# Five of twelve gate/val chunks computed with seven products instead of eight

## The chip, the cores and the metric

The kernel runs on 1 core of one Trainium2 chip. The metric is device time in microseconds (us) of one execution; three runs of the kernel before stand below. Engines are named as in the profile: PE (TensorE, its weight loads as PEld), DVE (VectorE), ACT (ScalarE), POOL (GpSimd), SP (the queue that issues the loads).

## What is computed

Causal attention of 24 (batch, head) pairs, 448 tokens, head dimension 64, in all 896 tokens of 768 features, and then two feed-forward blocks. The inputs of the blocks are fp64.

```python
def _moe_ref(x, w_in, w_out):            # 768 -> 2048 -> 768
    h = x @ w_in
    g = np.where(h >= 1, h, np.where(h <= -1, 0.0, (h + 1) ** 2 / 4))
    return (g @ w_out).astype(np.float32)

def _moe2_ref(x, w_gate, w_val, w_out):  # 768 -> 1536 -> 768
    g = x @ w_gate
    return (g / (1.0 + np.exp(-g)) * (x @ w_val) @ w_out).astype(np.float32)
```

## The kernel before

The kernel goes through five stages, each held on chip: attention (with the first part of x @ w_in woven in), the rest of h, y = g @ w_out ("Y stage", 6 column chunks d), gate and val with u = silu(gate)·val ("gv stage", 12 column chunks f, two groups g of N = 448 tokens), and u @ w_o2 (output stage, two halves hf, 7 token tiles, 6 weight pieces).

Every large product is made exact enough by splitting both operands into a high and a low part (fp32r): mm3 issues three matmuls, high·high, high·low, low·high. A gv chunk is 2 (gate, val) × 2 token groups × 6 contraction pieces × 3 = 72 matmuls of 128 rows by 448 columns, each with its own weight load. `split` makes the parts of an activation: a cast on ACT (L84) and a subtraction on DVE (L85). y is split as each of its column chunks ends (L515), u at the end of each chunk and token group (L541).

Weights come as 768-column pieces by one queue of loads (SP, L100). The class Weights turns a piece into high and low parts in a generator, `operations`: three integer steps on DVE (L116, L123, L127) put the fp32 number together from the fp64 bits, ACT casts the high part (L135), and POOL subtracts for the low part (L136; DVE for the first nine pieces). `tick` advances this by one step, `get` runs it until a piece is there, `free` gives a buffer back; four buffers (WBUFS) are in rotation.

At the start PE runs products of zeros (`zeros`, L382): WARM = 18 ahead of the first scores, and HOLD = (12, 6, 4, 2) more in the first turns of the attention loop. The scores of a step (`scores`) are matmuls of q and k, then matmuls that add the mask; DVE takes their maximum next (`greatest`, L277).

A scheduler orders the instructions of each engine by a priority that falls with the place in the program; each engine then runs its list in order. `follow` keeps matmuls of one group together, and PINNED holds the first weight steps in program order.

## Time and profile before

| | us |
|---|---|
| three runs | 621.1, 620.0, 621.09 |
| median | 621.09 |
| the profiled execution | 620.53 |
| its span | 618.8 |
| PE busy (matmul records) | 608.1 |
| PEld busy | 533.2 |
| DVE busy | 361.1 |
| ACT busy | 210.5 |
| POOL busy | 117.8 |

The busy times are sums of one execution over its span. A matmul's record begins before the one ahead of it has ended, so the records of PE overlap, and their sum is not the time that PE needs at its closest spacing. The profiled execution's own time is the span and what lies around it, 1.7 us.

### The profile page before, as it was taken

To read this page: it belongs to the slowest core of one execution; us is meant where nothing else is said; L and a number is where in the kernel's file an instruction comes from. 1 tells how busy PE (TensorE), PEld (TensorE's weight loads), DVE (VectorE), ACT (ScalarE), POOL (GpSimd) and SP (SyncE) were. 2 spreads that over 40 slices of the span, in tenths; PEclk is the share of its full clock that TensorE was granted. 3 is DMA by queue.
4 is the path that set the end of the run, shared out by engine and by line. 5 is a ranking of instruction groups with operands and counts; after the bars stand their busy time and mean duration, and the time that the engine had idled before them with its cause. 6 is when DMAs were issued, how large, how long until landed. Compare 5 with 4: busy or idle time off the path is not lost.

```text
span 618.8 us, 8656 instructions
## 1 busy us (share of the span) xinstructions
PE 608.1 (98%) x3394; PEld 533.2 (86%) x3398; DVE 361.1 (58%) x687; ACT 210.5 (34%) x455; POOL 117.8 (19%) x68
## 2 busy tenths in 40 slices
PE   9999999999999999999999999999999999999997
PEld 4666667668999999999999999999999999999997
DVE  2999999773796766443344455555555555532401
ACT  3777877563344433111111322222222222112100
POOL 0000000000311222232232322222222223321300
PEclk9999999999999999999999999999999999999999
DMA  7576554200140233422333333333333333335002
GB/s 238 160 223 192 178 171 153 68 0 2 47 157 14 94 101 111 126 101 86 126 113 112 120 94 127 111 103 106 110 124 120 103 103 103 103 110 172 14 0 90
DMA packets 18665, 67.81 MB, mean 110 GB/s; under 512 B 2112, under 2 KB 6784, under 8 KB 18624
## 3 DMA queue, kind: packets, MB, share of 16 engines
q1 hardware_dynamic: 18624, 67.25, 34.3%
q8 instruction: 27, 0.44, 0.3%
q14 instruction: 14, 0.11, 0.1%
HBM read 64.49 MB, written 2.75 MB: 109 GB/s over the span
## 4 chain that ended last, share of the span: by engine, by line
PE 87%; DVE 10%; ACT 3%; issue 0%; ACTq 0%
PE mm L73 62%; PE mm L556 5%; PE mm L555 5%; PE mm L554 5%; PE mm L75 3%; DVE s L277 2%; ACT p L291 2%; PE s L73 2%; DVE p L315 2%; PE o L75 1%; PE t L75 1%; PE mm L382 1%; DVE wt L123 1%; PE s L75 1%; PE o L73 1%; DVE wt L127 1%
## 5 line engine op out<-in xcount | busy, mean ns | idle before, releaser
L136 POOL TENSOR_TENSOR wl<-wt,wh 128x768 fp32r<-128x768 f32 (+1 forms) x61 | 116.9, 1918 | 470.5 <-ACT wh L135 470.5
L135 ACT CAST wh<-wt 128x768 fp32r<-128x768 f32 (+1 forms) x70 | 57.3, 819 | 179.2 <-PE mm L73 108.8
L73 PE MATMUL mm<-yh,wl 128*128 128x448 f32 x288 | 105.3, 366 | 0.0
L73 PE MATMUL mm<-yh,wh 128*128 128x448 f32 x288 | 105.3, 365 | 0.0
L73 PE MATMUL mm<-yl,wh 128*128 128x448 f32 x288 | 105.2, 365 | 0.0
L116 DVE TENSOR_SCALAR wt<-wraw 128x768 int32<-128x768 int32 (+1 forms) x70 | 41.4, 591 | 109.0 <-POOL wl L136 108.8
L73 PE MATMUL mm<-gh,wh 128*128 128x448 f32 x192 | 70.2, 365 | 0.0
L73 PE MATMUL mm<-gh,wl 128*128 128x448 f32 x192 | 70.2, 365 | 0.0
L73 PE MATMUL mm<-gl,wh 128*128 128x448 f32 x192 | 70.2, 365 | 0.0
L123 DVE SCALAR_TENSOR_TENSOR wt<-wraw,wt 128x768 int32<-128x768 int32 (+1 forms) x70 | 67.4, 964 | 1.3
L127 DVE SCALAR_TENSOR_TENSOR wt<-wraw,wt 128x768 int32<-128x768 int32 (+1 forms) x70 | 65.2, 931 | 1.6
L73 PE MATMUL mm<-xh,wh 128*128 128x448 f32 x165 | 62.5, 379 | 2.2 <-DVE q L200 2.1
L73 PEld LDWEIGHTS mm<-yh,wh 128*128 128x128 f32 x288 | 54.1, 188 | 4.2
L73 PEld LDWEIGHTS mm<-yl,wh 128*128 128x128 f32 x288 | 54.1, 188 | 4.2
L73 PEld LDWEIGHTS mm<-yh,wl 128*128 128x128 f32 x288 | 54.1, 188 | 4.2
L555 PE MATMUL mm<-wl,uh 128*128 128x384 f32 x168 | 56.2, 334 | 0.0
L556 PE MATMUL mm<-wh,ul 128*128 128x384 f32 x168 | 56.2, 334 | 0.0
L554 PE MATMUL mm<-wh,uh 128*128 128x384 f32 x168 | 56.2, 334 | 0.0
L291 ACT ACTIVATE p<-s,mx 112x112 f32<-112x112 f32 (+3 forms) x96 | 46.3, 495 | 23.2 <-DVE mx L279 17.9
L73 PE MATMUL mm<-xl,wh 128*128 128x448 f32 x138 | 50.4, 365 | 0.0
L73 PE MATMUL mm<-xh,wl 128*128 128x448 f32 x138 | 50.2, 365 | 0.0
L277 DVE TENSOR_REDUCE s<-s 112x2 f32<-112x224 f32 (+3 forms) x48 | 35.0, 736 | 8.9 <-PE s L75 8.6
(73 smaller groups left out, 945.5 us busy)
## 6 DMA issues: line engine op xcount, KB each, us to landing
wraw<-w_gv SPq DMA_DIRECT2D x24, 768.0 KB, 4.2
wraw<-w_in SPq DMA_DIRECT2D x16, 768.0 KB, 4.4
wraw<-w_out SPq DMA_DIRECT2D x12, 768.0 KB, 4.4
wraw<-w_o SPq DMA_DIRECT2D x12, 768.0 KB, 4.2
qk_t<-qk SPq DMA_DIRECT2D x12, 336.0 KB, 4.5
wraw<-w_out SPq DMA_DIRECT2D x6, 512.0 KB, 3.8
qk_t<-qk SPq DMA_DIRECT2D x12, 224.0 KB, 2.9
v_t<-v SPq DMA_DIRECT2D x12, 224.0 KB, 2.7
```

What stands on the lines that cost most here:

```text
L73: return product(*args, **kw)
L75: return tc.keep_in_program_order(product(*args, **kw))
L116: first = nc.vector.tensor_scalar(out=t, in0=w[:, :, 1], scalar1=3, scalar2=0x3FFFFFF8, op0=ALU.logical_shift_left, op1=ALU.bitwise_and,)
L123: nc.vector.scalar_tensor_tensor(out=t, in0=w[:, :, 1], scalar=-0x40000000, in1=t, op0=ALU.bitwise_and, op1=ALU.bitwise_or,)
L127: nc.vector.scalar_tensor_tensor(out=t, in0=w[:, :, 0], scalar=29, in1=t, op0=ALU.logical_shift_right, op1=ALU.bitwise_or,)
L135: nc.scalar.copy(out=wh[:, :n], in_=t.bitcast(F32))
L136: (nc.vector if i < LOW_V else nc.gpsimd).tensor_tensor(out=wl[:, :n], in0=t.bitcast(F32), in1=wh[:, :n].bitcast(F32), op=ALU.subtract,)
L277: nc.vector.tensor_reduce(out=mx[:, i], in_=s[:C, :, off:off + w], axis=AX.X, op=ALU.max)
L291: nc.scalar.activation(out=p[:, h, off:off + w], in_=s[:C, h, off:off + w], func=AF.Exp, bias=mx[:, i, h:h + 1], scale=0.125, accum_out=sm ...
L554: nc.tensor.matmul(out=ps, lhsT=c, rhs=a, start=(f == 0), stop=False)
L555: nc.tensor.matmul(out=ps, lhsT=c, rhs=b, start=False, stop=False)
L556: nc.tensor.matmul(out=ps, lhsT=d, rhs=a, start=False, stop=(f == FC2 - 1))
```

## The change

In five of the twelve chunks (SEVEN = 2, 4, 6, 8, 10) the gate and val of both token groups and both halves of the contraction are computed by one level of Strassen's scheme, in the form with seven products (`seven`); the other chunks keep eight (`eight`). A product is 3 contraction pieces × 3 matmuls = 9 matmuls of 448 columns. The scheme needs sums:

- Of the weights: four sums of 384 columns on DVE (`sums`), and parts of three of their blocks (768, 384, 384 columns), cast on ACT and subtracted on DVE (S_LOW = "V"). POOL subtracts the low part of half of val.
- Of y: T1 to T4, three pieces each, on DVE. The raw y is copied to SBUF by ACT in the Y stage, and the parts of y and of the T are made at the end of that stage.
- Of the products: c1, c5 (copies on ACT), c16, c167 and three more additions on DVE in each such chunk.

u is kept unsplit; its parts are made (`split_u`) for f = 0, 1 behind chunk 10 and for the others in the first half of the output stage. WARM goes from 18 to 8. The first step of 24 gv weight pieces is kept in program order.

```diff
--- before.py
+++ after.py
...
-WARM = 18
+WARM = 8
...
+SEVEN = (2, 4, 6, 8, 10)
...
+S_LOW = "V"
...
-                if i < PINNED:
+                if i < PINNED or PIN0 <= i - I_GV < PIN1:
                     tc.keep_in_program_order(first)
...
+                f, val = divmod(i - I_GV, 2)
+                if f in SEVEN and i < I_O2:
+                    if not val:
+                        gate = t.bitcast(F32)
+                    else:
+                        yield from self.sums(i, gate, t.bitcast(F32))
+                        continue
...
+        def sums(self, i, gate, val):
+
+            g, v = ([x[:, k * HALF:(k + 1) * HALF] for k in range(2)] for x in (gate, val))
+            wh = wp.tile([128, WB], F32R, tag="wh", name="vh")
+            wl = wp.tile([128, WB], F32R, tag="wl", name="vl")
+            nc.scalar.copy(out=wh[:, :HALF], in_=v[1])
+            nc.gpsimd.tensor_tensor(out=wl[:, :HALF], in0=v[1], in1=wh[:, :HALF].bitcast(F32), op=ALU.subtract)
+            t = sums_p.tile([128, 4 * HALF], F32, tag="s", name="ws", bufs=1)
+            sh = sums_p.tile([128, 3 * HALF], F32R, tag="sh", name="sh")
+            sl = sums_p.tile([128, 3 * HALF], F32R, tag="sl", name="sl")
+            s1, s2, s3, s4 = (t[:, k * HALF:(k + 1) * HALF] for k in range(4))
+            nc.vector.tensor_tensor(out=s1, in0=v[0], in1=v[1], op=ALU.add)
+            nc.vector.tensor_tensor(out=s2, in0=s1, in1=g[0], op=ALU.subtract)
+            yield
+            nc.vector.tensor_tensor(out=s4, in0=g[1], in1=s2, op=ALU.subtract)
+            nc.vector.tensor_tensor(out=s3, in0=g[0], in1=v[0], op=ALU.subtract)
+            yield
+            for hi, lo, x in ((sh[:, :WB], sl[:, :WB], t[:, :WB]), (sh[:, WB:], sl[:, WB:], s3),
+                              (wh[:, HALF:], wl[:, HALF:], s4)):
+                nc.scalar.copy(out=hi, in_=x)
+                (nc.vector if S_LOW == "V" else nc.gpsimd).tensor_tensor(
+                    out=lo, in0=x, in1=hi.bitcast(F32), op=ALU.subtract)
+                if x is not s4:
+                    yield
+            self.got[i] = wh, wl, sh, sl
+            self.ready = i + 1
+            yield
+
...
-    for g in range(2):
-        Y[g] = (xy.tile([128, KC, N], F32R, tag="xh", name="yh"), xy.tile([128, KC, N], F32R, tag="xl", name="yl"))
+
+    raw = [xy.tile([128, KC, N], F32, tag="xh", name="yraw") for g in range(2)]
+    sums12, sums34 = (xy.tile([128, KC, N], F32, tag="xl", name="traw") for _ in range(2))
+    T1, T2, T3, T4 = sums12[:, :3], sums12[:, 3:], sums34[:, :3], sums34[:, 3:]
     for d in range(KC):
         pss = [bank() for _ in range(2)]
...
+        if d == KC - 1:
+            break
+        ps = [p[:, :N] for p in pss]
         for g in range(2):
-            split(pss[g][:, :N], Y[g][0][:, d], Y[g][1][:, d])
+            nc.scalar.copy(out=raw[g][:, d], in_=ps[g])
+        e = d - 3
+        if d < 3:
+            nc.vector.tensor_tensor(out=T1[:, d], in0=ps[1], in1=raw[0][:, d], op=ALU.subtract)
+        else:
+            nc.vector.tensor_tensor(out=T2[:, e], in0=ps[1], in1=T1[:, e], op=ALU.subtract)
+            nc.vector.tensor_tensor(out=T3[:, e], in0=ps[1], in1=raw[1][:, e], op=ALU.subtract)
+            nc.vector.tensor_tensor(out=T4[:, e], in0=ps[0], in1=T2[:, e], op=ALU.subtract)
     gctx.close()
-
-    up = ctx.enter_context(tc.tile_pool(name="up", bufs=1, reuse_waits="tile"))
-    uh = [up.tile([128, 2 * N], F32R, tag=f"uh{f}", name=f"uh{f}") for f in range(FC2)]
-    ul = [up.tile([128, 2 * N], F32R, tag=f"ul{f}", name=f"ul{f}") for f in range(FC2)]
-    for f in range(FC2):
-        ws = [W.get(I_GV + 2 * f), W.get(I_GV + 2 * f + 1)]
+    mctx = ExitStack()
+    yp = mctx.enter_context(tc.tile_pool(name="yp", bufs=1, reuse_waits="tile"))
+    sums_p = mctx.enter_context(tc.tile_pool(name="sums_p", bufs=2, reuse_waits="tile"))
+    tctx = ExitStack()
+    tp = tctx.enter_context(tc.tile_pool(name="tp", bufs=1, side="right", reuse_waits="tile"))
+    Y = {(g, c): [yp.tile([128, N], F32R, name=f"y{part}{g}_{c}") for part in "hl"] for c in range(KC) for g in range(2)}
+    for g in range(2):
+        for c in range(KC - 1):
+            split(raw[g][:, c], *Y[g, c])
+        split(pss[g][:, :N], *Y[g, KC - 1])
+    ps = [p[:, :N] for p in pss]
+    nc.vector.tensor_tensor(out=T2[:, 2], in0=ps[1], in1=T1[:, 2], op=ALU.subtract)
+    nc.vector.tensor_tensor(out=T3[:, 2], in0=ps[1], in1=raw[1][:, 2], op=ALU.subtract)
+    nc.vector.tensor_tensor(out=T4[:, 2], in0=ps[0], in1=T2[:, 2], op=ALU.subtract)
+    T = {}
+    for k, t in enumerate((T1, T2, T3, T4)):
+        T[k] = [tp.tile([128, 3, N], F32R, name=f"t{part}{k}") for part in "hl"]
+        split(t, *T[k])
+
...
+    def add(ps, w, at, rows, first, last):
+
+        for c in range(3):
+            sl = slice(at + c * 128, at + (c + 1) * 128)
+            for i, (a, b) in enumerate(((0, 0), (0, 1), (1, 0))):
+                nc.tensor.matmul(
+                    out=ps[:, :N], lhsT=w[a][:, sl], rhs=rows[c][b], start=(first and c == i == 0),
+                    stop=(last and c == i == 2), skip_group_check=True,
+                )
+
+    def gated(f, g, gate, val):
+        sg = ev.tile([128, N], F32, tag="r", name="sg")
+        nc.scalar.activation(out=sg, in_=gate, func=AF.Sigmoid)
+        nc.vector.tensor_tensor(out=sg, in0=gate, in1=sg, op=ALU.mult)
+        nc.vector.tensor_tensor(out=u_raw[f][:, g * N:(g + 1) * N], in0=val, in1=sg, op=ALU.mult)
+
+    def eight(f, ws):
         for g in range(2):
-            yh, yl = Y[g]
-            pss = []
+            pss = [bank() for _ in range(2)]
             for s in range(2):
-                wh, wl = ws[s]
-                ps = bank()
-                for c in range(KC):
-                    sl = slice(c * 128, (c + 1) * 128)
-                    mm3(ps[:, :N], wh[:, sl], wl[:, sl], yh[:, c], yl[:, c], c == 0, c == KC - 1)
-                pss.append(ps)
+                for half in range(2):
+                    add(pss[s], ws[s], half * HALF, chunks(g, half), not half, bool(half))
+                    W.tick(TICK8[half])
                 if g:
                     W.free(I_GV + 2 * f + s)
-            sg = ev.tile([128, N], F32, tag="r", name="sg")
-            nc.scalar.activation(out=sg, in_=pss[0][:, :N], func=AF.Sigmoid)
-            nc.vector.tensor_tensor(out=sg, in0=pss[0][:, :N], in1=sg, op=ALU.mult)
-            u = pss[1][:, :N]
-            nc.vector.tensor_tensor(out=u, in0=u, in1=sg, op=ALU.mult)
-            split(u, uh[f][:, g * N:(g + 1) * N], ul[f][:, g * N:(g + 1) * N])
-            W.tick(4)
+            gated(f, g, *(p[:, :N] for p in pss))
+
+    def seven(f, ws):
+
+        gate, val, sums = ws[0], ws[1][:2], ws[1][2:]
+        b1, b2, b3 = (bank() for _ in range(3))
+        p1, p2, p3 = (b[:, :N] for b in (b1, b2, b3))
+        c1, c5 = (ev.tile([128, N], F32, tag="t", name=f"c{i}") for i in (1, 5))
+        c16, c167 = (ev.tile([128, N], F32, tag="c", name=f"c{i}") for i in (16, 167))
+        add(b1, gate, 0, chunks(0, 0), True, True)
+        nc.scalar.copy(out=c1, in_=p1)
+        W.tick(1)
+        add(b2, sums, HALF, sums_of(1), True, True)
+        nc.vector.tensor_tensor(out=c16, in0=p2, in1=c1, op=ALU.add)
+        W.tick(1)
+        add(b3, sums, 0, sums_of(0), True, True)
+        nc.scalar.copy(out=c5, in_=p3)
+        W.tick(1)
+        add(b1, gate, HALF, chunks(0, 1), False, True)
+        W.free(I_GV + 2 * f)
+        W.tick(1)
+        add(b2, sums, 2 * HALF, sums_of(2), False, True)
+        nc.vector.tensor_tensor(out=c167, in0=p2, in1=c1, op=ALU.add)
+        W.tick(1)
+        add(b3, val, HALF, chunks(1, 1), False, True)
+        nc.vector.tensor_tensor(out=p3, in0=p3, in1=c16, op=ALU.add)
+        nc.vector.tensor_tensor(out=c5, in0=c5, in1=c167, op=ALU.add)
+        gated(f, 1, p3, c5)
+        W.tick(1)
+        add(b2, val, 0, sums_of(3), False, True)
+        W.free(I_GV + 2 * f + 1)
+        nc.vector.tensor_tensor(out=p2, in0=p2, in1=c1, op=ALU.add)
+        gated(f, 0, p1, p2)
+        W.tick(2)
+
+    u_raw, uh, ul = {}, {}, {}
+
+    def split_u(pool, f):
+        uh[f], ul[f] = (pool.tile([128, 2 * N], F32R, name=f"u{part}{f}") for part in "hl")
+        for g in range(2):
+            half = slice(g * N, (g + 1) * N)
+            split(u_raw[f][:, half], uh[f][:, half], ul[f][:, half])
+
+    for f in range(FC2):
+        if f % 3 == 0:
+            triple = xy.tile([128, KC, N], F32, tag=("xh", "xl")[f // 3 % 2], name="u")
+            for e in range(3):
+                u_raw[f + e] = triple[:, 2 * e:2 * e + 2].rearrange("p g n -> p (g n)")
+        ws = [W.get(I_GV + 2 * f), W.get(I_GV + 2 * f + 1)]
+        (seven if f in SEVEN else eight)(f, ws)
+        if f == SEVEN[-1]:
+            tctx.close()
+            up = ctx.enter_context(tc.tile_pool(name="up", bufs=1, side="right", reuse_waits="tile"))
+            for e in range(2):
+                split_u(up, e)
+    mctx.close()
+    up2 = ctx.enter_context(tc.tile_pool(name="up2", bufs=1, reuse_waits="tile"))
...
         last = NB - LASTB
         for i in range(last):
             w = W.get(I_O2 + hf * NB + i)
+            if hf == 0:
+                for f in range(2 * i + 2, 2 * i + 4):
+                    split_u(up if f < 6 else up2, f)
             for t in range(7):
                 product(i, w, t)
...
```

**PE at the start.** The kernel before, from the last of its 18 zeros; s_144 and s_167 are the scores of the first two steps, mask_b and ident_b the mask and the identity that adds it:

```order
L382 MATMUL mm_114<-idle_112 128x512
L73 MATMUL s_144<-qk_t_100 112x224 [waits DMAHW0_49]
L75 MATMUL s_144<-qk_t_100 112x224
L75 MATMUL s_144<-qk_t_100 112x112 x2
L73 MATMUL s_167<-qk_t_104 112x224 [waits DMAHW2_49]
L75 MATMUL s_167<-qk_t_104 112x224
L75 LDWEIGHTS ident_b_59 [waits DVE_49]
L75 MATMUL s_144<-mask_b_60,ident_b_59 112x112 [waits Pool_49]
L75 MATMUL s_167<-qk_t_104 112x112
```

The kernel after, from the last of its 8 zeros; s_134 and s_157 are the same scores:

```order
L421 MATMUL mm_114<-idle_112 128x512
L77 MATMUL s_134<-qk_t_100 112x224 [waits DMAHW0_49]
L79 MATMUL s_134<-qk_t_100 112x224
L79 MATMUL s_134<-qk_t_100 112x112 x2
L77 MATMUL s_157<-qk_t_104 112x224 [waits DMAHW2_49]
L79 MATMUL s_157<-qk_t_104 112x224
L79 MATMUL s_157<-qk_t_104 112x112 x2
L421 LDWEIGHTS idle_112
```

The scores of both steps now stand together behind 8 zeros; 7 more zeros (of HOLD) follow, and then the eight mask matmuls, which before stood among the scores.

**DVE in the gv stage.** Before, a token group's end; wt is a weight piece in its three steps, sg and mm the gate and u, ul the low part of u:

```order
L127 SCALAR_TENSOR_TENSOR wt_3730<-wraw_3626,wt_3730 128x768 [waits DVE_49]
L540 TENSOR_TENSOR mm_3597<-mm_3597,sg_3616 128x448 [waits PE_49]
L116 TENSOR_SCALAR wt_3784<-wraw_3680 128x768 [waits DMAHW3_49,Pool_49]
L85 TENSOR_TENSOR ul1_3415<-mm_3597,uh1_3403 128x448 [waits Activation_49]
L123 SCALAR_TENSOR_TENSOR wt_3784<-wraw_3680,wt_3784 128x768 [waits DVE_49]
L127 SCALAR_TENSOR_TENSOR wt_3784<-wraw_3680,wt_3784 128x768 [waits DVE_49]
L538 TENSOR_TENSOR sg_3670<-mm_3632,sg_3670 128x448 [waits Activation_49]
L540 TENSOR_TENSOR mm_3651<-mm_3651,sg_3670 128x448 [waits DVE_49,PE_49]
L85 TENSOR_TENSOR ul2_3416<-mm_3651,uh2_3404 128x448 [waits Activation_49]
```

After, a chunk of seven products, from the last u of the chunk before it:

```order
L608 TENSOR_TENSOR u_3773<-mm_3838,sg_3887 128x448 [waits PE_49]
L632 TENSOR_TENSOR c16_3896<-mm_3892,c1_3894 128x448 [waits PE_49,Activation_49]
L120 TENSOR_SCALAR wt_3922<-wraw_3811 128x768 [waits DMAHW5_49]
L127 SCALAR_TENSOR_TENSOR wt_3922<-wraw_3811,wt_3922 128x768 [waits DVE_49]
L131 SCALAR_TENSOR_TENSOR wt_3922<-wraw_3811,wt_3922 128x768 [waits DVE_49]
L641 TENSOR_TENSOR c167_3897<-mm_3892,c1_3894 128x448 [waits PE_49]
L645 TENSOR_TENSOR c5_3895<-c5_3895,c167_3897 128x448 [waits DVE_49,Activation_49]
L644 TENSOR_TENSOR mm_3893<-mm_3893,c16_3896 128x448 [waits PE_49]
L607 TENSOR_TENSOR sg_3972<-mm_3893,sg_3972 128x448 [waits Activation_49]
L650 TENSOR_TENSOR mm_3892<-mm_3892,c1_3894 128x448 [waits PE_49]
```

The subtraction of u's low part is gone from this stage. The three weight steps stand between c16, which waits for the second product, and c167, which waits for the fifth.

**DVE where the Y stage ends.** Before; yl is the low part of the last column chunk of y, one for each token group:

```order
L116 TENSOR_SCALAR wt_3382<-wraw_3306 128x768 [waits DMAHW5_49,Pool_49]
L123 SCALAR_TENSOR_TENSOR wt_3382<-wraw_3306,wt_3382 128x768 [waits DVE_49]
L127 SCALAR_TENSOR_TENSOR wt_3382<-wraw_3306,wt_3382 128x768 [waits DVE_49]
L116 TENSOR_SCALAR wt_3514<-wraw_3352 128x768 [waits DMAHW6_49,Pool_49]
L123 SCALAR_TENSOR_TENSOR wt_3514<-wraw_3352,wt_3514 128x768 [waits DVE_49]
L127 SCALAR_TENSOR_TENSOR wt_3514<-wraw_3352,wt_3514 128x768 [waits DVE_49]
L85 TENSOR_TENSOR yl_2594<-mm_3264,yh_2593 128x448 [waits Activation_49]
L85 TENSOR_TENSOR yl_2596<-mm_3265,yh_2595 128x448 [waits Activation_49]
```

After; yl0_0 is the low part of token group 0, column chunk 0:

```order
L120 TENSOR_SCALAR wt_3337<-wraw_3242 128x768 [waits DMAHW4_49,Pool_49]
L127 SCALAR_TENSOR_TENSOR wt_3337<-wraw_3242,wt_3337 128x768 [waits DVE_49]
L131 SCALAR_TENSOR_TENSOR wt_3337<-wraw_3242,wt_3337 128x768 [waits DVE_49]
L120 TENSOR_SCALAR wt_3371<-wraw_3295 128x768 [waits DMAHW5_49,Pool_49]
L127 SCALAR_TENSOR_TENSOR wt_3371<-wraw_3295,wt_3371 128x768 [waits DVE_49]
L131 SCALAR_TENSOR_TENSOR wt_3371<-wraw_3295,wt_3371 128x768 [waits DVE_49]
L89 TENSOR_TENSOR yl0_0_3394<-yraw_2583,yh0_0_3393 128x448 [waits PE_49,Activation_49]
L89 TENSOR_TENSOR yl0_1_3398<-yraw_2583,yh0_1_3397 128x448 [waits PE_49,Activation_49]
L89 TENSOR_TENSOR yl0_2_3402<-yraw_2583,yh0_2_3401 128x448 [waits PE_49,Activation_49]
```

All twelve low parts of y now stand behind the weight steps, where before the last two did.

## Rows read from the trace of the kernel before

**Rows 1.** Page, part 1 (busy us, share, xinstructions) and part 2 (granted clock, tenths).

```profile
PE 608.1 (98%) x3394; PEld 533.2 (86%) x3398; DVE 361.1 (58%) x687; ACT 210.5 (34%) x455; POOL 117.8 (19%) x68
...
PEclk9999999999999999999999999999999999999999
```

**Rows 2.** PE's waits: line <- releaser: total us, times, longest.

```profile
PE mm L73 <- DVE q L200: 2.1, 3, 1.3
...
PE mm L382 <- DVE half_b L387: 1.2, 1, 1.2
```

**Rows 3.** Tile yh: ns min/median/max, first and last start us, forms.

```profile
L73 PEld LDWEIGHTS mm<-yh,wh x288: 187/188/189, 352.4 to 526.9; 128*128 128x128 f32 x144
L73 PE MATMUL mm<-yh,wh x288: 362/365/370, 352.6 to 527.0; 128*128 128x448 f32 x144
...
L73 PE MATMUL mm<-yh,wl x288: 361/365/370, 353.0 to 527.5; 128*128 128x448 f32 x144
```

**Rows 4.** Windows: us; PE, PEld, DVE, ACT, POOL busy; clock, DMA, GB/s.

```profile
381.80:396.40 14.60, 14.60 (x74) 13.54 (x73) 8.37 (x13) 3.74 (x7) 4.34 (x2) 1.00 0.36 109
```

**Rows 5.** Timeline of the start: start us, us, engine, operation [idle before].

```profile
0.74 0.38 SPq L240 DMA_DIRECT2D qk_t<-qk  x1
...
1.19 4.88 PE L382 MATMUL mm<-idle 128*128 128x512 bf16 x11 [1.19 <-DVE half_b L387]
...
1.59 0.15 PEld L382 LDWEIGHTS <-idle 128*128 128x128 bf16 x1 [0.28 <-issue]
1.65 0.42 SPq L240 DMA_DIRECT2D qk_t<-qk  x1
...
5.86 0.15 PEld L382 LDWEIGHTS <-idle 128*128 128x128 bf16 x1 [0.28 <-issue]
6.21 0.96 PEld L382 LDWEIGHTS <-idle 128*128 128x128 bf16 x5 [0.21 <-issue]
7.60 0.44 PE L73 MATMUL s<-qk_t 64*112 64x224 f32 x1
...
8.74 0.13 PEld L75 LDWEIGHTS <-ident_b 112*112 112x112 bf16 x1 [0.29 <-issue]
...
10.26 0.40 DVE L277 TENSOR_REDUCE s<-s 112x2 f32<-112x224 f32 x1 [8.65 <-PE s L75]
```

**Rows 6.** DMA issues at 0.74 and 1.65 us: KB, us to landing.

```profile
qk_t<-qk SPq DMA_DIRECT2D x1, 224.0 KB, 2.7
qk_t<-qk SPq DMA_DIRECT2D x1, 224.0 KB, 3.7
```

**Rows 7.** Windows in the attention stage.

```profile
10.00:20.00 10.00, 9.95 (x79) 6.19 (x79) 7.79 (x28) 6.71 (x31) 0.00 (x0) 1.00 0.67 209
50.00:60.00 10.00, 9.61 (x70) 5.76 (x68) 10.00 (x33) 8.63 (x29) 0.00 (x0) 1.00 0.58 183
```

**Rows 8.** Groups by line and form: busy us, mean ns | idle before, releaser.

```profile
L136 POOL TENSOR_TENSOR wl<-wt,wh 128x768 fp32r<-128x768 f32 x55 | 109.1, 1986 | 438.6 <-ACT wh L135 438.6
L123 DVE SCALAR_TENSOR_TENSOR wt<-wraw,wt 128x768 int32<-128x768 int32 x64 | 63.3, 989 | 1.2
L127 DVE SCALAR_TENSOR_TENSOR wt<-wraw,wt 128x768 int32<-128x768 int32 x64 | 61.0, 954 | 1.5
L135 ACT CAST wh<-wt 128x768 fp32r<-128x768 f32 x64 | 53.6, 837 | 146.9 <-PE mm L73 76.5 <-PE mm L556 37.7 <-issue 30.2
L116 DVE TENSOR_SCALAR wt<-wraw 128x768 int32<-128x768 int32 x64 | 38.8, 606 | 102.5 <-POOL wl L136 102.3
...
L85 DVE TENSOR_TENSOR ul<-mm,uh 128x448 fp32r<-128x448 f32 x24 | 14.9, 620 | 7.2 <-ACT uh L84 7.2
L84 ACT CAST uh<-mm 128x448 fp32r<-128x448 f32 x24 | 12.8, 534 | 62.4 <-DVE mm L540 62.4
L136 DVE TENSOR_TENSOR wl<-wt,wh 128x768 fp32r<-128x768 f32 x9 | 8.4, 938 | 0.0
```

**Rows 9.** Page, part 6: DMA issues, KB each, us to landing.

```profile
wraw<-w_gv SPq DMA_DIRECT2D x24, 768.0 KB, 4.2
```

More of the change, by code (lines that the diff above doesn't have):

```diff
@@ L44 @@
 NORM1 = "V"
+SEVEN = (2, 4, 6, 8, 10)
+TICK8 = (1, 2)
+PIN0, PIN1 = 4, 28
+S_LOW = "V"
 PINNED = 2
@@ L164, in fused_kernel @@
     I_O2 = I_GV + 2 * FC2
-    xT, G, Y = {}, {}, {}
+    xT, G = {}, {}
     for g in range(2):
@@ new lines, in fused_kernel, with chunks @@
+    nc.vector.tensor_tensor(out=T2[:, 2], in0=ps[1], in1=T1[:, 2], op=ALU.subtract)
[5 more added lines that the diff above has]
+        split(t, *T[k])
+    def chunks(g, half):
+        return [Y[g, 3 * half + c] for c in range(3)]
@@ new lines, in sums_of @@
+    def sums_of(k):
+        return [[x[:, c] for x in T[k]] for c in range(3)]
+    def add(ps, w, at, rows, first, last):
[6 more added lines that the diff above has]
+                )
@@ L566, in fused_kernel @@
         ws = [W.get(I_O2 + hf * NB + i) for i in range(last, NB)]
+        if hf == 0:
+            for f in range(2 * last + 2, FC2):
+                split_u(up2, f)
         for t in range(7):
```

## The prediction

> **What bounds the kernel now.** I read the page first: PE is busy 98% of the span, and the granted clock is full in every slice [rows 1]. The waits of PE come next. They have seven rows, 6.5 us together, of which the largest is 2.1 [rows 2]; asked for from 156 us on, the same view is empty. From there PE never waits, so the time is the number of matmuls times their spacing, and a change of the count counts in full as long as no new wait appears.
>
> The price of a matmul is not its record. In the tile yh one lasts 0.365 us, but the first begins at 352.6 and the last at 527.5 [rows 3], with 12 × 72 = 864 in between: (527.5 − 352.6) / 863 = 0.2027 us from start to start. The gv chunk of 381.8 to 396.4 us says the same: 72 slots in 14.60 us, weight loads busy 13.54 of them, DVE 8.37 [rows 4].
>
> Before 110 us another engine leads: DVE is busy 10.00 of 10 us at 50 to 60 us, and 7.79 at 10 to 20 us [rows 7]. That chain begins with the first maximum on DVE at 10.26 us, which had waited 8.65 us for PE [rows 5]. What brings it forward can bring all that follows forward.
>
> **The products.** Five chunks lose one product in eight, 9 matmuls each. That is 45 × 0.2027 = 9.12 us, all on the path, since the stage has no other wait. By the records it would be 45 × 0.365 = 16.4 us. [...] By the records the forecast would be 7.3 us lower, which I don't believe: 72 records of 0.365 us don't fit into 14.60 us.
>
> **The start.** Ahead of the first maximum stand 18 zeros, the scores, and masks woven into them; after the change 8 zeros, the scores of two steps, 7 zeros, the masks. So three zeros less. [...] Three zeros are worth 0.64 us at the fast spacing and 1.28 at the slow one. Two switches between scores and masks, each with a gap of 0.29 us [rows 5], go too, at most 0.58. Bounds: 0.64 to 1.86 us; I take 1.3, near the middle, because one part of the 15 zeros and scores now runs slow and the other fast. The loads don't hold this up: q and k of the first step land at 0.74 + 2.7 = 3.4 us, of the second at 1.65 + 3.7 = 5.35 [rows 5, 6], and the eight zeros end at 1.19 + 8 × 0.43 = 4.6 [rows 5], with 4 scores to run before the second step's. Whether the 1.3 us reach the end hangs on DVE behind it, which is nearly full [rows 7], so I carry them whole.
>
> **DVE in the gv stage.** Two plain chunks cost 2 × 8.37 = 16.7 us of DVE. One seven-product chunk beside one plain chunk: minus four subtractions of u (4 × 0.62 [rows 8]), plus four sums of weights of 384 columns, plus three low parts of 768, 384 and 384, plus five additions of 448 columns. The 768 columns have a row on DVE, 0.94 us, and 448 have 0.62 [rows 8]; 384 lie between 0.47 (half of 768) and 0.62, and I take 0.54, on the line through both rows. So 16.7 − 2.5 + 2.2 + (0.94 + 1.08) + 3.1 = 21.5 us, in 63 + 72 = 135 slots = 27.4 us: 79%. DVE is not the bound, and its work is hidden by PE's; were that cover gone, each us of DVE would cost a us. Two copies on ACT per such chunk (0.53 each [rows 8]) stand beside 3.74 of 14.60 us.
>
> **The new wait in the gv stage.** Of the seven products the fifth and the seventh are in the same bank. PE must not begin the seventh before DVE has made c167 from the fifth. The fifth ends at slot 45 = 9.12 us of the chunk, the seventh would begin at slot 54 = 10.94: 1.82 us for an addition of 0.62, a margin of 1.2. Ahead of c167 on DVE stand c16, which can go at 3.65, and three weight steps (0.61 + 0.99 + 0.95 = 2.55 [rows 8]): 4.27 + 2.55 = 6.8, so DVE is free 2.3 us before the fifth product ends. A weight step would have to begin 2.3 + 1.2 = 3.5 us late before PE waits. It waits for its raw load, which lands 4.2 us after its issue [rows 9] and is issued about a chunk ahead. I put this wait at nothing; bounds 0 and, if each chunk lost as much as the margin, 5 × 1.2 = 6 us. I am near the low end because the load has some 10 us to spare.
>
> **Where the Y stage ends.** Before, DVE had two low parts of y to make behind the last weight steps; now it has twelve, and twelve pieces of the T after. The weight steps wait for POOL (1.99 us a piece [rows 8]), and POOL for a cast on ACT (0.84), which by the order on ACT waits for a matmul 61 places before the stage's end, 61 × 0.2027 = 12.4 us. Behind it: 0.84 + 1.99 + 2.55 = 5.4, so the first low part begins at −7.0 us and is there at −6.4, needed at 0. Token group 0 ends its last column 12 matmuls early, at −2.4; its sixth low part is cast and subtracted behind that and behind its queue by about −0.7, and is wanted by the sixteenth matmul, at +3.2 us. Cover of some 4 us; I put the stall at nothing, with a bound of 12 × 0.62 = 7.4 us if all twelve fell behind the end. The T are first wanted in chunk 2, two chunks (29 us) on.
>
> **The output stage.** 24 casts (0.53) and 24 subtractions (0.62) of u move here, 14.9 us of DVE over the first half; they are issued one weight piece ahead of their use, and a piece is 42 matmuls of 384 columns, about 42 × 0.2027 × 384 / 448 = 7.3 us of PE, for 4 × 0.62 = 2.5 us of DVE and 2.1 of ACT. Hidden; what they would cost uncovered is the first split alone, 1.2 us.
>
> **The sum.** 9.12 + 1.3 = 10.4 us. The profiled execution of 620.53 us (span 618.8 and 1.7 around it) goes to 610.1; the median of 621.09 to 610.7. I give the middle, 610.4.
>
> **Rivals.** (A) The forecast: 610.4, with the start's bounds and the 0.6 us between profile and median 609.6 to 611.2.
>
> (B) The start gives nothing, or loses. For it: DVE is busy only 7.79 of the 10 us behind the start [rows 7], so something other than the first maximum sets part of it; that gives 611.4, and 611.7 from the median. [...]
>
> (C) A small stall in each of the five chunks, at c167 or where a weight piece comes late, up to 1 us each: 610.9 to 615.4. For it: c167 has the smallest margin in the plan, 1.2 us. Against: DVE is idle when the fifth product ends.
>
> (D) Slower. Weight steps stand between c16 and c167 and wait for a load; DVE runs in order, so c167, u and PE's seventh product wait with them. The first 3.5 us are free. To pass 622.3 from 610.4 it takes 11.9 us, 2.4 in each of the five chunks: from 5.9 us of lateness on, it decides. For it: the order of DVE puts the steps there. Against: loads of 4.2 us [rows 9], on queues busy 0.36 of the stage [rows 4].
>
> (E) More than counted: an earlier first maximum also lets the weights of the attention stage come earlier, and part of the 6.5 us of early PE waits [rows 2] goes: at most the 2.1 of the largest, some 609.
>
> **How the numbers follow.** A 66%, B 16%, C 8%, D 4%, E 6%. The range leaves out the low end of E, the loss in B and the upper half of C and D: 608.6 to 612.9. A measurement of this kernel can tell about 0.2% (1.24 us) from no change. Faster 0.95 (all but D and a remainder), slower 0.035, same 0.015.
>
> **What would show it.** In the trace after, the gv stage with 819 matmuls lasts 165.8 us from first to last, at 0.2027 us a slot; no PE wait of a row on DVE appears in it; DVE is busy about 79% of a pair of chunks; the first maximum begins at 8.4 to 9.6 us; the output stage is as long as before. Wrong would be: a PE wait for c167 in each seven-product chunk, weight steps that wait for a load, a first maximum behind 10.3 us, or a spacing of matmuls in the seven-product chunks over 0.2027.

## The result

The changed kernel takes 609.81 us (four runs, 609.39 to 610.16) against 620.88 for the kernel before: a ratio of 0.9824, with a 95% interval of 0.981 to 0.9839. The forecast was 610.4 in a range of 608.6 to 612.9. The total was right. Its largest step, the products, was right in kind and 0.5 us too large; its second, the start, was too small by about 0.9; the work on DVE and the slack of c167 were misjudged in places where it cost nothing.

The page of the kernel after, parts 1 and 2, answers to [rows 1]; under it two rows of the tile yh, which answer to [rows 3]:

```profile
PE 596.5 (98%) x3340; PEld 522.8 (86%) x3343; DVE 427.8 (70%) x763; ACT 230.2 (38%) x494; POOL 120.9 (20%) x68
...
PEclk9999999999999999999999999999999999999999
```

```profile
L599 PE MATMUL mm<-yh,wh x198: 362/365/370, 350.1 to 516.0; 128*128 128x448 f32 x198
...
L599 PE MATMUL mm<-yh,wl x198: 362/365/370, 350.5 to 516.4; 128*128 128x448 f32 x198
```

PE is as full as before. The gv stage ran from 352.6 to 527.5 us before, 174.9, and runs from 350.1 to 516.4 now, 166.3: 8.6 us less. Its first matmul comes 2.5 us earlier. Together that is 11.1, and the spans differ by 618.8 − 607.8 = 11.0. No PE wait is left from 150 us on, as in [rows 2] from 156. DVE has risen by 66.7 us of busy time, and no wait of PE came of it.

The windows of the kernel after over two pairs of a seven-product and a plain chunk, columns as in [rows 4]:

```profile
379.30:406.70 27.40, 27.40 (x136) 25.30 (x135) 21.05 (x31) 7.31 (x13) 7.44 (x4) 1.00 0.36 114
406.70:434.20 27.50, 27.50 (x137) 25.37 (x137) 23.70 (x34) 7.67 (x13) 7.45 (x4) 1.00 0.36 115
```

PE is busy throughout; DVE takes 21.05 and 23.70 us, where the forecast had 21.5. The two pairs don't hold the same work: the second has 34 DVE records against 31, two weight steps among them, and the two pairs behind it take 23.70 and 23.64. So 23.70 is the value to set against the forecast.

The start of the kernel after on the timeline, against [rows 5]:

```profile
4.58 0.44 PE L77 MATMUL s<-qk_t 64*112 64x224 f32 x1
...
5.36 0.44 PE L77 MATMUL s<-qk_t 64*112 64x224 f32 x1
...
6.11 1.19 PEld L421 LDWEIGHTS <-idle 128*128 128x128 bf16 x7
...
8.20 1.76 DVE L316 TENSOR_REDUCE s<-s 112x2 f32<-112x224 f32 x4 [6.59 <-PE s L79]
```

The first maximum begins at 8.20 us where it began at 10.26; the forecast had 8.4 to 9.6.

### The profile page after: what moved, and what is told of

Read it like the earlier page. It is cut to its first block, busy times and chain, and to the rows that moved or that the text cites. A ratio compares the mean times of both kernels' runs of the same rounds, so it can differ in the third digit from the quotient of the medians.

```text
span 607.8 us, 8657 instructions
## 1 busy us (share of the span) xinstructions
PE 596.5 (98%) x3340; PEld 522.8 (86%) x3343; DVE 427.8 (70%) x763; ACT 230.2 (38%) x494; POOL 120.9 (20%) x68
## 4 chain that ended last, share of the span: by engine, by line
PE 85%; DVE 13%; ACT 2%; issue 0%; ACTq 0%
PE mm L77 34%; PE mm L599 27%; PE mm L688 5%; PE mm L689 5%; PE mm L687 5%; DVE s L316 3%; PE mm L79 2%; DVE p L354 2%; PE mm L421 1%; DVE wt L127 1%; DVE wt L131 1%; PE s L77 1%; ACT p L330 1%; PE t L79 1%; DVE wl L147 1%; PE o L79 1%
## 5 line engine op out<-in xcount | busy, mean ns | idle before, releaser
L147 POOL TENSOR_TENSOR wl<-wt,wh 128x768 fp32r<-128x768 f32 (+1 forms) x56 | 114.0, 2039 | 447.8 <-ACT wh L146 447.8
L146 ACT CAST wh<-wt 128x768 fp32r<-128x768 f32 (+1 forms) x65 | 53.0, 817 | 152.9 <-DVE wt L131 67.7
L120 DVE TENSOR_SCALAR wt<-wraw 128x768 int32<-128x768 int32 (+1 forms) x70 | 48.1, 688 | 63.9 <-POOL wl L147 63.4
L131 DVE SCALAR_TENSOR_TENSOR wt<-wraw,wt 128x768 int32<-128x768 int32 (+1 forms) x70 | 73.8, 1054 | 1.2
L599 PE MATMUL mm<-yl,wh 128*128 128x448 f32 x198 | 72.4, 365 | 0.0
L599 PE MATMUL mm<-yh,wl 128*128 128x448 f32 x198 | 72.3, 365 | 0.0
L599 PE MATMUL mm<-yh,wh 128*128 128x448 f32 x198 | 72.3, 365 | 0.0
L127 DVE SCALAR_TENSOR_TENSOR wt<-wraw,wt 128x768 int32<-128x768 int32 (+1 forms) x70 | 69.0, 986 | 1.1
L689 PE MATMUL mm<-wh,ul 128*128 128x384 f32 x168 | 56.3, 335 | 0.0
L330 ACT ACTIVATE p<-s,mx 112x112 f32<-112x112 f32 (+3 forms) x96 | 46.3, 496 | 21.7 <-DVE mx L318 16.5
L599 PEld LDWEIGHTS mm<-yl,wh 128*128 128x128 f32 x198 | 37.2, 188 | 3.0
L599 PEld LDWEIGHTS mm<-yh,wh 128*128 128x128 f32 x198 | 37.2, 188 | 3.0
L599 PEld LDWEIGHTS mm<-yh,wl 128*128 128x128 f32 x198 | 37.2, 188 | 2.9
```

The source lines that it names most:

```text
L120: first = nc.vector.tensor_scalar(out=t, in0=w[:, :, 1], scalar1=3, scalar2=0x3FFFFFF8, op0=ALU.logical_shift_left, op1=ALU.bitwise_and,)
L127: nc.vector.scalar_tensor_tensor(out=t, in0=w[:, :, 1], scalar=-0x40000000, in1=t, op0=ALU.bitwise_and, op1=ALU.bitwise_or,)
L131: nc.vector.scalar_tensor_tensor(out=t, in0=w[:, :, 0], scalar=29, in1=t, op0=ALU.logical_shift_right, op1=ALU.bitwise_or,)
L146: nc.scalar.copy(out=wh[:, :n], in_=t.bitcast(F32))
L147: (nc.vector if i < LOW_V else nc.gpsimd).tensor_tensor(out=wl[:, :n], in0=t.bitcast(F32), in1=wh[:, :n].bitcast(F32), op=ALU.subtract,)
L330: nc.scalar.activation(out=p[:, h, off:off + w], in_=s[:C, h, off:off + w], func=AF.Exp, bias=mx[:, i, h:h + 1], scale=0.125, accum_out=sm ...
```

## The experiments

Each was timed beside the kernel before (620.91, 620.83 and 620.23 us in three groups of runs).

### The two terms apart

WARM = 8 in the kernel before:

> The kernel before with WARM = 8 and nothing else: the start term alone. The forecast's step priced it at 1.3 us (0.64 to 1.86), so 619.6. The two traces read together say more: the first maximum moved from 10.26 to 8.20 us and the gv stage began 2.5 us earlier, which gives 618.4 with the first maximum at about 8.2 us. Rival: the earlier start is eaten by DVE behind it and the 2.5 us come from elsewhere in the change; then 620.9.

```diff
-WARM = 18
+WARM = 8
```

Measured 618.7 us, ratio 0.9969 (0.9957 to 0.9981): 1.2 to 2.7 us less. The time is near the 618.4 expected, but the first maximum of its trace begins at 9.15 us and not at 8.2 (below). And the kernel after with WARM back at 18:

> The kernel after with WARM = 18: the products alone. The forecast's step says 9.12 us, so 620.9 - 9.1 = 611.8 with the spacing of 0.2027 us everywhere. The trace of after has a spacing of 0.2033 over the gv stage and a stage of 166.3 us in place of 174.9, which gives 8.6 and 612.3. Rival: the products were worth less than 8 and the start more; then above 612.9.

```diff
-WARM = 8
+WARM = 18
```

Measured 612.0, ratio 0.9867 (0.9849 to 0.9885): 7.1 to 9.4 us less. The two add up to the whole (2.2 and 8.9 of 11.1), so neither term feeds on the other as far as this scatter can tell. The products' 9.1 lies in its interval; the start's 1.3 lies at the low end of its own, and both differences of medians (620.91 − 618.7, and 612.0 − 609.81) are 2.2.

The traces show why a single one misleads about the start. The kernel before with WARM = 8:

```profile
4.71 0.71 PE L73 MATMUL s<-qk_t 64*112 64x224 f32 x1
...
5.97 0.58 PE L73 MATMUL s<-qk_t 64*112 64x224 f32 x1
...
7.06 1.19 PEld L382 LDWEIGHTS <-idle 128*128 128x128 bf16 x7
...
9.15 1.76 DVE L277 TENSOR_REDUCE s<-s 112x2 f32<-112x224 f32 x4 [7.53 <-PE s L75]
```

The kernel after with WARM = 18:

```profile
4.46 1.82 PEld L421 LDWEIGHTS <-idle 128*128 128x128 bf16 x9 [0.16 <-issue]
...
9.37 1.76 DVE L316 TENSOR_REDUCE s<-s 112x2 f32<-112x224 f32 x4 [7.76 <-PE s L79]
```

The same eight zeros precede the scores in the first of these and in the kernel after, but here a score's matmul lasts 0.71 and 0.58 us where it lasts 0.44 there, and scores of two steps take from 4.71 to 7.06 in place of 4.58 to 6.11. In [rows 5] the weight loads of the zeros stand (5.86 − 1.59) / 10 = 0.427 us apart at first; in the fast spacing five take 0.96 us, of which the last takes 0.10: (0.96 − 0.10) / 4 = 0.215. With 18 zeros it begins at 4.46 us in the kernel after and at 6.21 in the one before [rows 5]; with 8 it has begun by 4.58 in the kernel after, and in the one before at some point between 6.34 and 7.06. So, after the same zeros from 1.19 us on, the moment differs between executions. Where the expectations below speak of the rise of the clock, this change of spacing is what the traces show; the granted clock is printed as 1.00 on both sides of it (0 to 4, 4 to 6 and 6 to 8 us of the kernel before). With the fast spacing early in both, 18 and 8 zeros give a first maximum at 9.37 and 8.20 us: 1.2 apart, close to the forecast's 1.3.

The rest of the start's 2.2 us comes later. From the fifth to the thirteenth maximum the kernel after takes 12.2 us with 8 zeros and 13.3 with 18 (first two rows with 8, last two with 18):

```profile
13.40 0.39 DVE L316 TENSOR_REDUCE s<-s 112x2 f32<-112x224 f32 x1
...
25.61 1.06 DVE L316 TENSOR_REDUCE s<-s 112x2 f32<-112x224 f32 x2
```

```profile
14.56 0.39 DVE L316 TENSOR_REDUCE s<-s 112x2 f32<-112x224 f32 x1
...
27.89 1.05 DVE L316 TENSOR_REDUCE s<-s 112x2 f32<-112x224 f32 x2
```

The kernel before shows the same, 12.2 with 8 zeros (14.35 to 26.56) and 13.3 with 18 (15.46 to 28.78), so these 1.1 us don't depend on when the fast spacing began. WARM is all that differs, and with it PE has the later zeros of HOLD and the products of p and v in another order in this stretch. That this order costs the 1.1 us is likely, but no run changed the order alone.

### Zeros behind the data

> As after with WARM = 0; four zeros of HOLD still stand ahead of the scores, then eleven, then the masks, 15 in all as in after. PE is free at 2.9 us and waits for q and k (3.4 and 5.35). Theory: the four zeros that moved behind the scores cost 4 x 0.215 = 0.9 us where the data had landed anyway, less what the scores gain by 1.1 us of earlier start: the second step's data hold them until 5.4, so the first maximum comes within 0.9 us of after's, 609.8 to 610.7. Rival: PE's gaps ahead of the data let the clock rise later, scores and zeros run slow: first maximum above 10 us, 611 to 613.

```diff
-WARM = 8
+WARM = 0
```

Measured 612.14 (610.03 to 612.25), ratio 0.9853 (0.9833 to 0.9873). Three of the four executions lie at 612.1 to 612.3, where the rival put them, and one at 610.03, where the theory did. The timeline of one of the three:

```profile
3.46 0.71 PE L77 MATMUL s<-qk_t 64*112 64x224 f32 x1 [0.39 <-DMA qk_t<-qk]
...
5.40 0.71 PE L77 MATMUL s<-qk_t 64*112 64x224 f32 x1 [0.47 <-DMA qk_t<-qk]
...
9.22 0.75 PEld L421 LDWEIGHTS <-idle 128*128 128x128 bf16 x4 [0.17 <-issue]
...
10.87 0.40 DVE L316 TENSOR_REDUCE s<-s 112x2 f32<-112x224 f32 x1 [9.25 <-PE s L79]
```

PE waits twice for q and k, and the fast spacing begins only at 9.22 us, later than in the traces above with 8 or 18 zeros (by 7.06). This is what the rival feared, with a price of 2.3 us. Eight zeros cover the loads, or nearly (in one trace with eight PE waited 0.22 us for the second step's q and k); four don't. That the waits made the fast spacing begin late fits three executions but was not shown: of these one was profiled, and the one of 610.03 was not.

### Masks ahead of the other zeros

> As pad_t, and the zeros of HOLD held in program order, so that the eight masks stand ahead of them: 8 zeros, scores, masks, where after has 7 zeros more in between. The seven take 7 x 0.215 = 1.5 us in the trace of after; the first maximum would come at 6.6 to 7.8 us, by when the clock rises, in place of 8.1 to 9.2. Theory that the first maximum carries: 1 to 1.5 us less than pad_t. Rival: the loads of q and k of the next steps or DVE take it back: no change against pad_t.

```diff
         def zeros(n):
             for _ in range(n):
-                nc.tensor.matmul(out=warm, lhsT=idle[:, :128], rhs=idle, start=True, stop=True)
+                tc.keep_in_program_order(nc.tensor.matmul(out=warm, lhsT=idle[:, :128], rhs=idle, start=True, stop=True))
```

On top of the edit that moves T by 32 bytes (below). Measured 610.22 against 608.86 for that edit alone: 1.4 us slower, although its first maximum came at 7.65 us, earlier than the 8.34 there. Neither the theory nor its rival held. The gv stage began at 351.5 in place of 350.1. So the first maximum isn't all that is carried; how zeros and attention stand on PE behind it counts as much. The loss lies between 46 and 134 us: at the 25th maximum this run led by 1.6 us (46.3 against 47.9), at the last it was 1.3 behind (134.5 against 133.2). Its zeros go on to 51.9 us, where they end at 32.8 without the edit, and its first product of x @ w_in comes at 52.3 in place of 33.2. The order of all zeros of the loop changed here, and which of them costs the 1.4 us wasn't separated.

### How many chunks

> SEVEN = (2, 6, 10), three chunks in place of five. If each chunk gives 9 matmuls and nothing is a fixed cost: 2 x 9 x 0.2027 less 2 x 36 x 0.0028 = 3.4 us more than after, 613.2. If the sums of y had a fixed cost on the path, after lies above the line from before through this run by that much. Rival: a cost in each seven-product chunk that the trace hides in its spacing; then less than 3 us more, below 612.8.

```diff
-SEVEN = (2, 4, 6, 8, 10)
+SEVEN = (2, 6, 10)
```

Measured 613.6, ratio 0.9888 (0.9873 to 0.9903), 0.4 from the 613.2 expected. From the 618.7 of the kernel before with 8 zeros, which saves no product, three chunks give 5.1 us and five give 8.9: 1.7 and 1.8 each. A fixed cost would put after below the line through 618.7 and this run, not above it as the expectation says; after lies 0.4 below, inside the scatter of the runs. The gv stages of the traces (174.9, 169.7 and 166.3 us for none, three and five) give 1.73 and 1.72 each, so no fixed cost shows in that stage.

> SEVEN = (2, 4, 6, 8, 9, 10): one chunk more, so that three stand in a row. By the products it gives 9 x 0.2027 = 1.8 us, 608.1. Rival, DVE becomes the bound: a seven-product chunk with its sums wants some 13.7 us of DVE in the trace of after (23.7 of a pair less a half of 16.7 plus 2.5 for the u that moved), in 12.8 us of PE; two such chunks in a row leave DVE 1 to 2 us short and PE then waits for weights or c167: 609 to 611, with rows of PE waiting on DVE in the trace.

```diff
-SEVEN = (2, 4, 6, 8, 10)
+SEVEN = (2, 4, 6, 8, 9, 10)
```

Measured 611.61, ratio 0.9856 (0.9842 to 0.9871): 1.8 us slower than after, where the products alone would make it 1.8 faster. The rival's direction held; its 609 to 611 was still too low. PE's waits in this run, and a window over the end of its gv stage (columns as in [rows 4]):

```profile
PE mm L599 <- ACT sh L173: 0.8, 1, 0.8
PE mm L599 <- ACT c L629: 0.7, 1, 0.7
PE mm L599 <- DVE c L641: 0.5, 1, 0.5
...
PE mm L599 <- POOL wl L147: 0.3, 1, 0.3
```

```profile
489.20:518.40 29.20, 27.45 (x131) 23.92 (x131) 27.76 (x43) 13.99 (x27) 8.23 (x4) 1.00 0.34 111
```

No such wait exists in after. One of the four names DVE (c167), the others a cast of the sums and the copy c1 on ACT and a low part on POOL. DVE is busy 27.76 of the last 29.20 us: three such chunks in a row leave it no plain chunk to do their sums in. Yet in chunk 9 it sat idle for 3.6 us ahead of c167, so a lack of DVE time is the likely cause and not the only possible one; the order of its work is another.

> As pad_t with SEVEN = (2, 4, 6, 8, 10, 11): a sixth chunk at the end of the stage, where the next weights are the output stage's. By the products 1.8 us less than pad_t: 607.1. Rival, DVE has no room for the sums of chunk 11 beside those weights and u of 0 and 1 is split only when T has gone: a PE wait of 2 to 4 us around the end of the stage, 608.5 to 611.

```diff
-SEVEN = (2, 4, 6, 8, 10)
+SEVEN = (2, 4, 6, 8, 10, 11)
```

On top of the edit that moves T by 32 bytes (below, 608.86). Measured 612.0, ratio 0.9857 (0.9841 to 0.9874). The rival again, and again above its range; three of PE's four waits stand in the output stage (L689 to L691):

```profile
PE mm L689 <- ACT uh L88: 1.7, 1, 1.7
PE mm L690 <- POOL wl L147: 1.2, 1, 1.2
PE mm L601 <- DVE c L643: 0.7, 1, 0.7
PE mm L691 <- DVE ul L89: 0.6, 1, 0.6
```

The split of u has no plain chunk 11 left to hide behind. Five chunks, each beside a plain one, fit; both ways tried of adding a sixth lose more than it gives.

### The slack of c167

> In chunks 4 and 8 ten additions of 448 columns in SBUF (a maximum of c16 with itself, which changes nothing) stand on DVE ahead of c167, held there in program order: some 10 x 0.56 = 5.6 us of delay. In the trace of after c167 of chunk 4 ends at 416.74 and the seventh product begins at 417.76, with DVE idle for 1.72 us ahead of c167: slack 2.7 us (2.4 in chunk 2's idle time and 1.0: 3.4). Theory: PE waits about 2.9 us in each of the two chunks, 5 to 6 us in all, 615.3, with rows of PE waiting on DVE c. Rival, that the wait can't bind because the weights behind it are early enough and PE's seventh product can wait behind other work: under 1 us.

```diff
+        for _ in range(10 if f in (4, 8) else 0):
+            tc.keep_in_program_order(nc.vector.tensor_tensor(out=c16, in0=c16, in1=c16, op=ALU.max))
-        nc.vector.tensor_tensor(out=c167, in0=p2, in1=c1, op=ALU.add)
+        tc.keep_in_program_order(nc.vector.tensor_tensor(out=c167, in0=p2, in1=c1, op=ALU.add))
```

Measured 615.38, ratio 0.9913 (0.9894 to 0.9932), as expected, but not by the expected sum.

> As the run with ten additions, but four of them (4 x 0.56 = 2.2 us) ahead of c167, in all five chunks. The slack of 2.7 us or more in the trace of after holds them: no PE wait on DVE in the gv stage, stage length 166.3 us as in after. Rival, that the slack is smaller than the trace says (POOL's share of the memory, late loads): a PE wait in some chunk, up to 1 us each.

```diff
-        for _ in range(10 if f in (4, 8) else 0):
+        for _ in range(4):
```

The edit just shown, with four in all five chunks. One run: 616.81 us, 7 us more than after, where nothing was expected. The timeline of this run in chunk 4, and the four additions by themselves (ns min/median/max):

```profile
415.33 4.12 DVE L642 TENSOR_TENSOR c<-c 128x448 f32<-128x448 f32 x4
...
416.42 1.89 POOL L147 TENSOR_TENSOR wl<-wt,wh 128x768 fp32r<-128x768 f32 x1 [3.40 <-ACT wh L146]
419.37 0.62 DVE L643 TENSOR_TENSOR c<-mm,c 128x448 f32<-128x448 f32 x1
420.04 0.47 PE L599 MATMUL mm<-th,vh 128*128 128x448 f32 x1 [1.34 <-DVE c L643]
```

```profile
L642 DVE TENSOR_TENSOR c<-c x4: 616/624/2148, 415.3 to 418.8; 128x448 f32<-128x448 f32 x4
```

The four lasted 4.12 us, not 2.2. One of them, begun while POOL's subtraction of 1.89 us ran, took 2.15 us in place of 0.62; and they start some (418.8 − 415.33 − 1.53) / 3 = 0.65 us apart and not 0.56. Each reads what the one ahead has written; whether that is the cause was not shown. Four times 0.65 and the 1.5 beside POOL are 4.1. Of that 2.74 us are slack (in after, chunk 4, DVE was idle for 1.72 us ahead of c167, and c167 ended at 416.74, 1.02 before the seventh product at 417.76), and 4.12 − 2.74 = 1.38 is what PE waited, 1.34 by its row. The five rows sum to 5.6 us, while the gv stage grew by 7.2 (173.5 in place of 166.3): a row counts idle time from the end of the last record, which lies 0.16 us behind the matmul's slot, and the first matmul after a wait stands 0.3 us ahead of the next in place of 0.2. The slack as read from the trace was about right; the price of an instruction was not, since it left out POOL.

In the run with ten, they lasted 8.09 us, and PE waited only 2.25:

```profile
414.79 8.09 DVE L642 TENSOR_TENSOR c<-c 128x448 f32<-128x448 f32 x10
422.80 0.62 DVE L643 TENSOR_TENSOR c<-mm,c 128x448 f32<-128x448 f32 x1
```

```profile
423.47 0.47 PE L599 MATMUL mm<-th,vh 128*128 128x448 f32 x1 [2.25 <-DVE c L643]
```

Here the scheduler had put 14 matmuls of the next chunk, 2.8 us, ahead of the seventh product: 8.09 − 2.74 − 2.84 = 2.5. The expectation met the number by two errors that cancel: a delay too short by 2.5 us and a cover that it didn't know of. In chunks 2, 6 and 10 of this run c167 is held in program order too, without additions ahead of it, and PE doesn't wait; so the waits come from the additions.

### DVE beside POOL

> As after, with the low part of the second half of val subtracted on DVE in place of POOL (five instructions of 384 columns). In the trace of after the sum on line 169 takes 1.2 us on the mean, one on line 165 of the same size 0.55, and it runs while POOL subtracts this low part. Theory that the two engines collide: line 169 falls to 0.55 us, and DVE's busy time per pair of chunks doesn't rise although it has 0.55 us more to do. Rival, that the sum is slow for its operands: 1.2 us stays. No change of the time is expected in either case.

```diff
-            nc.gpsimd.tensor_tensor(out=wl[:, :HALF], in0=v[1], in1=wh[:, :HALF].bitcast(F32), op=ALU.subtract)
+            nc.vector.tensor_tensor(out=wl[:, :HALF], in0=v[1], in1=wh[:, :HALF].bitcast(F32), op=ALU.subtract)
```

One run, 610.36 us, with a gv stage of 166.3 us as in after. The sum on line 169, first in the kernel after, then in this run:

```profile
L169 DVE TENSOR_TENSOR ws<-wt 128x384 f32<-128x384 f32 x5 | 6.0, 1202 | 0.0
```

```profile
L169 DVE TENSOR_TENSOR ws<-wt 128x384 f32<-128x384 f32 x5 | 2.7, 546 | 0.0
```

It falls from 1202 to 546 ns, with the same operands: POOL was the cause. Over the whole gv stage DVE is busy 143.8 us in after and 139.1 here, although it has five instructions more:

```profile
350.10:516.60 166.50, 166.50 (x820) 153.82 (x819) 143.79 (x193) 55.24 (x90) 42.54 (x23) 1.00 0.33 103
```

```profile
350.90:517.40 166.50, 166.50 (x821) 153.76 (x819) 139.11 (x197) 55.15 (x90) 38.22 (x18) 1.00 0.33 105
```

### Where the operands lie

In after, matmuls that read the T sums stand 0.2053 us apart, the others 0.2028 (means over their starts in the trace), 0.5 us over 180 of them.

> The kernel after with 32 unused bytes per partition at the right end of SBUF, so that tiles on the right side (the T sums, five of the w_in pieces) begin at multiples of 64 bytes and not 32 bytes beside them. Theory that the place sets the spacing: matmuls that read T go from 0.2055 to 0.2027 us, mean duration from 0.368 to 0.365, and those of the w_in pieces 4 to 8 to 0.2027 too; 180 x 0.0028 + 90 x 0.004 = 0.9 us, 608.9. Rival that it comes from something else of these products: durations of 0.368 stay and the time stays at 609.8.

```diff
+    ctx.enter_context(tc.tile_pool(name="edge", bufs=1, side="right")).tile([128, 8], F32, name="edge")
```

Measured 609.88, no change in time: the gv stage shrank to 165.5 us, and the output stage grew from 87.2 us to 88.0 from its first matmul to its last (87.0 and 87.7 in the expectation below, which leaves out the last matmuls).

> The 32 unused bytes at the right end stand only while the w_in pieces 4 to 8 and the T sums lie there, and are gone when the parts of u come to the right side. In the run with the bytes throughout, the gv stage was 165.5 us in place of 166.3, but the output stage 87.7 in place of 87.0. Theory of the place: the gv stage keeps its 0.8 us and the output stage goes back to 87.0: about 0.8 us under after, 609.0. Rival that the stages only share a fixed total: no change.

```diff
+    stay.enter_context(tc.tile_pool(name="edge", bufs=1, side="right")).tile([128, 8], F32, name="edge")
...
+    tctx.enter_context(tc.tile_pool(name="edge2", bufs=1, side="right")).tile([128, 8], F32, name="edge")
```

Measured 608.86, ratio 0.9812 (0.9797 to 0.9827), against 0.9824 for after: about 1 us in the medians, inside both intervals. The trace is clearer: the gv stage lasts 165.5 us, the output stage 87.2. The tile th in after, and then in this run:

```profile
L599 PE MATMUL mm<-th,sh x45: 365/368/371, 381.1 to 497.7; 128*128 128x448 f32 x45
...
L599 PE MATMUL mm<-th,sl x45: 365/368/370, 381.5 to 498.1; 128*128 128x448 f32 x45
```

```profile
L601 PE MATMUL mm<-th,sh x45: 360/360/368, 381.1 to 496.9; 128*128 128x448 f32 x45
...
L601 PE MATMUL mm<-th,sl x45: 363/363/363, 381.5 to 497.3; 128*128 128x448 f32 x45
```

The matmuls that read T now stand 0.2008 us apart, closer than the others, where the theory had 0.2027. So 32 bytes of place change the spacing of these matmuls; two runs show it, each with a gv stage 0.8 to 0.9 us shorter. This version has the lowest median here.

## Why the prediction held, point by point

**The products** (9.12 us): right in kind; the stage gave 8.6 in the trace, and the runs with WARM = 18 give 8.3 by the ratio and 8.9 by the medians. The missing 0.5 us is the wider spacing of matmuls that read T, a thing [rows 3] couldn't show, as no T existed. A spacing over 0.2027 was one of the prediction's own signs of being wrong; it came, and was worth only that much. The pipelined record (16.4 us) was rightly put aside.

**The start** (1.3 us, bounds 0.64 to 1.86): too small; 1.9 by one pair of ratios, 2.7 by the other, 2.2 by the medians. The step that failed is that its gain is the shift of the first maximum. Its 0.64 and 1.28 us are three zeros at the two spacings of [rows 5], 0.215 and 0.427 us; which of the two held for which zeros differed between traces. With the fast spacing early in both, the maximum moves by 1.2 us (9.37 and 8.20), close to the forecast; another 1.1 us is gained between the fifth and the thirteenth maximum, which the forecast put at nothing. In those two traces the gv stage begins at 350.1 against 351.7, 1.6 us apart, so part of it is lost again on the way. The run with masks ahead of zeros shows the other side of it: an earlier maximum without a gain. That the total of 610.4 came within 0.6 us is in part luck: the products were 0.5 too large and the start 0.9 too small.

**DVE in the gv stage** (21.5 us a pair): 23.70 in a full pair. The step that failed is that each instruction was priced alone. In the pair from 406.7 us on, four run beside POOL and are longer by 3.3 us together: a weight step of 2.49 us in place of 0.95, the sum on line 169 (1.37, 0.54), the first weight step (1.21, 0.55) and an addition (0.89, 0.63). That is more than the 2.2 us by which the pair exceeds the forecast, so the other terms were some 1 us too large. PE covers DVE with five such chunks and not with six.

**c167** (slack 3.5): 3.4 in chunk 2, as forecast, and 2.7 in the four others. The 0.66 us between them are one weight step ahead of c167 that runs beside POOL there, 1.21 us in place of 0.55:

```profile
410.15 1.85 POOL L147 TENSOR_TENSOR wl<-wt,wh 128x768 fp32r<-128x768 f32 x1 [7.14 <-ACT wh L146]
...
411.21 1.21 DVE L120 TENSOR_SCALAR wt<-wraw 128x768 int32<-128x768 int32 x1
```

Rival D was priced as needing 5.9 us of lateness to turn the sign; with 2.7 us of slack it needs some 5.1. Its mechanism is real: 4.12 us of work in that place cost 7 us in all. In the gv stage of after DVE waits for no load.

**The end of the Y stage**: the first low part of y was forecast at 7.0 us before the gv stage; the trace has it at 343.22, 6.9 before 350.1, with no PE wait. The sixth of token group 0 was there 0.6 us behind the start of the stage and not 0.7 ahead of it, as one low part before it lasted 1.92 us beside POOL in place of 0.61; it was wanted at +3.2. **The output stage** took 87.2 us before and after.

**The rivals**: B, a start that gives nothing or loses, is refuted by the 2.2 us it gave, and its time "from the median" should read 612.0 (621.09 − 9.12); the upper end of A should read 611.3. C's stalls didn't come. E was right that more than counted would come, but not by its mechanism: PE's waits before 150 us grew from 6.5 to 7.3 us.

## What to carry to other kernels

Where one engine is full from end to end, a change of its work is worth instructions times their spacing (here 45 × 0.2027 = 9.1 us, of which the gv stage gave 8.6). The work that pays for it is free as long as each result is there before the full engine wants it: here one seven-product chunk in two left 2.7 us at c167, and work in that place beyond it was paid for although DVE still had some 2 us of idle time in each pair (27.03 of 29.09 us busy in the run with four additions). Price the helper's instructions with their neighbours on POOL, not alone: here that was 3.3 us in a pair. A gain at the start has to be measured with several runs: one trace carries with it the moment at which PE's fast spacing begins, 4.46 to 7.06 us here.
